# Rows of eight attention units loaded ahead into buffers that the dense layers have not yet filled, with a new written-out order

## The chip, the cores and the metric

The kernel runs on one core of a Trainium2 chip. The metric is the device time of one execution in microseconds (us). The engines work side by side, each through its own list of instructions: TensorE (PE, matmuls), VectorE (DVE), ScalarE (ACT), GpSimd (POOL) and SyncE (SP, which here only issues transfers). They wait for one another through semaphores.

## The reference

```python
# q, k, v: (8, 8, 576, 64); x: (4608, 512); w_in: (512, 2048); w_out: (2048, 512)
def attn(q, k, v):
    # 1: rows averaged in groups of 4, softmax attention over the 144 averages, result repeated 4 times
    # 2: softmax attention of each row over the rows with |i - j| < 4
    return out_up + out_local
x = attn(q, k, v).transpose(0, 2, 1, 3).reshape(4608, 512)
h = x @ w_in
out = (h - tanh(h)) @ w_out
```

All of it is float32 outside; the kernel casts to bf16 ahead of its matmuls.

## The kernel before

**Units.** Attention runs in 32 units. Unit p is the head pair p % 4 of batch p // 4. For each unit SP issues two loads of 256 KB (`load_qk`, L341: rows of k and of q, four sequence rows on one partition, into a buffer `st`) and two of 160 KB (`load_v`, L365: overlapping row windows of v for the two heads, into a buffer `vst`). The last 64 rows of q and k of a whole batch come in two loads of 128 KB (`sr`, L353), those of v in one (`vr`, L380). There are 4 buffers `st` and 5 buffers `vst`: unit p takes p % 4 and p % 5, so a load waits until the casts of the unit that had the buffer have read it.

**A unit's steps.** `st` is cast to bf16 (`qr`, L499; the last rows `rr`, L489), turned on PE for units 0 to 7 (L506) and by a transposing transfer on SP's queue from unit 8 on (L550; last rows L544), and pooled (L598 to L602, L613, L587, L592). `prep_v` casts `vst` (`vw`, L425), PE pools it (L456, units 0 to 11). PE makes the scores (L650, L660, L666), ACT the exponentials (L671 to L679), DVE or POOL the band mask (L706), PE the outputs (L720), DVE the division (L736, L738). The result goes back through PE (L763) or a transfer (L775) and is joined into `xT` (L756).

**Dense layers.** Block kb is one batch's 512 tokens. `mm1` (L797) multiplies `w_in` with `xT`, ACT takes tanh (L809) and DVE subtracts into `gT` (L812), two buffers by the block's parity. Block 0 multiplies `gT` with `w_out` directly (`mm2`, L878); blocks 1 to 7 use seven half products (L1018) on sums of `w_out` (`Tw`, four tiles, L927) and of `gT` (`S0` and others, L953). The weights come in 8 chunks of 1 MB issued by POOL (L406, L410).

**Order.** Nothing is scheduled on the chip or by the compiler. `Plan.emit` issues all operations in the order of the string `TURNS`; `ENGINES` says which engine takes an operation that has a choice, `BANKS` which PSUM bank, `FILL` where PE runs matmuls whose result is not used (L1227), and `BEHIND` adds waits between operations that share a port. Each engine works strictly in its own part of that order, and an SP transfer that has to wait holds back all that stand behind it on SP.

Of the kernel before, what the change touches and what calls it, by code (L numbers as in the profile page):

```python
# [7 lines left out]
FP32 = mybir.dt.float32  # L8
# [93 lines left out]
def kernel(  # L102
# [13 lines left out]
    NP = H // 2  # L116
# [38 lines left out]
        "000E0F0I0J06020B0M0N030K0L0G0H0401050O0P0Q0R0D0A0W0X0U0V0e0f101d1e11131B0g0h1512141f1g16"  # L155
        "171H1P0Y0Z180C0S0T1I1J1Q0k0l1C1A1L1K19220c0d1M1D1R1S091N1T1u231w0i0j1U2R1O1V240a0b252T26"
        "2G2H1v1j1k08291x1y2Z1l1m27200y1W0o0p071z1E2S1n1o2y2a280m0n1F2U211X1G2b1Y2c2X1Z2V1p1q2d39"
        "0z2I2J2z2W1r5H2n2o1a2Y1s2p2q0q0r3A1b2A2g1c1h1i0s0t3B2B3N3O2e2C3D33303P3Q3C2O1t2t2u3E312P"
        "2D2M2N0u0v3F3G352v2E2f5I2w363H325J343I5L3J37385P5K2K2L5M2h5N2Q5S5O2i2j5U665Q3K5R2F682k5E"
        "3L5v3M2l5T632m5x5V3d5F5X3j643k5y3p5w3q3r5B3s5C613e5D5z3t3v3w5W3l603m3f623u3g3T3U655Y3n3x"  # L160
        "3h0w0x3o6e3y6g3i412r2s426U43475Z3z6c4D3R3S5a444849456T674E6b46694F4G5g5h6B4A406d5b4B4J4K"
        "5c3V3W4P5d4H4L4M4C4Q3X3Y4R5k5l4N6V4I6X5e5f6W4S4V6Y4b5m5n6Z6f4O4T4c4d6a4e2x4h4U7A4i4j4f4W"
        "6A4X4Y4g5s4Z4k4n4o4l4a4t4u5G4v5t4z4w3Z3a4m6C6h6j556i506D4p6E4x514q526Q4r4y7D536F4s567B7F"
        "576G586H7f3b3c6R8854597C7g895A728d7E5u6k7I71967G6l976m7H6y8e6z8E8j8F8k737J76779C7K6n7L7l"
# [24 lines left out]
        "LnQyOgLvLzLoM0RTNfRDRELiM6NyOeOfR0M7LwM1RBRCMCMDM8M2O3O4QoMLMEM9O9OAMMOqOXOYOZMFMNOvRURV"
        "QuP0MOQzP1OoOkOiOjP6OlNZNaOrQvOhOsNXNYR1P9RFRGOpOwOmSJSKOxOtPER9RAOnR2RYPFRlRmPKOuOyO5O6"  # L190
        "P2PPRWP3RHRIP7R3P4RnRoOzV1PARXV2PBP5RNPGR4PHRZR5PCPLPIPSS4PDR6R7PMPTPJPNRaRORPRQPUPYRzRb"
        "PdPVRtPZPORyPeRcPaPRP8S0S1PWPfS5PlRePbPmSURpRqPXOBPgV3RLRMS6PnPqOcOdSWS7PvPoSNSOPrRdRrRs"
        "PwPsMSMTQ3RuPxQ4PtR8PcQ5PyQ8PhQ9Q6SPQFQAV5RfSRSSSAQBQGSVQKS2RgSQSZSaQLQHSdQPQMQIQQRvRwRx"
        "PjRhPiSXSYPkS3PpQNQYV6SLSMPuQRSeQES8PQQZPzSfQaQ1QSQ0V7V8ShQ2QpQ7QbQCVUSjRiRjQJSgS9QOQTSH"
        "SISbRRSBQDVBMHMIQdV9QUSqSrT6VAVCSCTTSDQeScQXSiSESFQcQhTRQfQiT7TUVTT8SyQjTZSzTaVZQgVDT9VE"
        "VVVWVOTETSUbVFTFVHSsStUcTgQkQlTGTHThSkTMVGTwV4TPTQTxSlVPSmTNTOU2VaU3VQVRUhRkU8VIVXSnSoUA"
        "VJVYVuUBVKUGUHTfVvVbUMTiSGVfTjVoVcUOVpToUPVdSpVqVrSTTpVwTvT2T0T1VxT3SuSvVeUiVySwSxUUT4Vz"
        "UVVLVMTuVgT5UNVsTAW0UaTBTIVmVhViTJVnTVTKU9TWUnVjVkW1TXTLUqTCW9UoUpUrVtTbQVQWTDTcWAW2TkW3"
        "TdTlW7UwTYTmWBVNTnUxWDTqWCTeVSW4W5TyUyTrWFW8U4WETsTzUCTtVlU0WGU1U5UDW6WHWIUIUEUJU6UQUFWJ"
        "WKURUKU7UWUXULUzV0USUdUYUTUeUjUfUZWLUsUkUgUtWSUuWXUlWcUvWMUmWTWUWQWYWNWZWRWeWaWfWOWmWsWV"  # L200
        "WPWdWxWWWiX4WbWgX5WtWhWkWyXAWzWnWuWlX0XFWoXGWjWpXNWqX6XOXSX7XXWvXPWrWwXHXBXIXYXCXfXZXTXD"
        "XkXaXgXlXQXrXhXwY1X1XiX3XUX8XqXVY2X2XxX9XEXvXJXsXyYAYBXmXzXLXMXnXRXWY0XbYOY3YFXcXdXtY4Y5"
        "XKXeY6YPXjXuXoYbYCY9YGYdYHXpYEYJYDY7Y8YQYKYIYRYSYLYTYUYcYMYNYVYeYWYfYiYgYZYaZ2YXYYYjYkYw"
        "YxZ3YyZ4YhYzYlZ0YmYnZ5Z1YoYpZ7YqZ6YrZAZ8Z9YvYsZBYtYuZCZDZJZEZKZHZFZGZOZIZPZQZRZSZLZMZN"
    )
    ENGINES = (
        "DDDDADDAAPPDAAPADADADDDDPDDDDDADPDAPDPDDAADPADAAAPADAAADDDDDDAPAADAAPPPDDDPPADAAAPPPPDAA"
        "PPADADPPPPDDPPPPAAPPPPDAAAADPPDADDAADDDDAPPPDDPPDADAPPAAPPDDAAPPPAAPPDDPPADDDDDPPDAPPAAP"
        "PDPDDAPPAAPPDPPPADPAADPDDPPADPPAADDDDPPDDDDDPPPAPPAADPDPDPAPPAADDDPDDAPPAAPPDDPPAPPPAAPD"
        "PDPPADDDDDPPPAPPAADPDPDDAPPAAPPDPDPADPAADDDPPPAPPPAADDDPPDDDDDDPPPAPPAAPPDPPPAPPDAPPDDPD"  # L210
        "APPAAPDDDPPAPPPDAPDDDDPADDDDDPPPAPPAAPPDPDPPDPAAPPDPPPDPAAPPDPPPPPDPDPPPDADDDDD"
    )
    BANKS = (
        "0123456017206457012760113005223301301030203210230101210031212003321100112311002032011320"
        "3101102201310203110023210201301001012110130100113200123101231023110021010131032110321321"
        "0301120310120031021101001002101021130203110032103213120130120310120120012010112030110210"
        "1010030210301230102310230123674512365714327601524736120"
    )
    FILL = (
        "13715 1771 1L61 1w31 2431 1E01 1X72 3351 3H21 2h72"  # L220
    )
    BEHIND = (
        "1B11 2S0y 5H0z 2f3F 655W 7A6a AmAF AnAL BiAs EgCZ DFFo JSFt IvGb IrJ6 MYJN MfJc NBKu QmL"
        "A LqNn NcNr O8OQ RYOp V1P7 SUS5 R8Ru Q0PQ VPVG VuRk VpVo UNVz VlWE"
# [60 lines left out]

    P = Plan(TURNS, ENGINES, BANKS, FILL, BEHIND)
# [51 lines left out]
    def load_qk(p):  # L338
        b, h0, s = p // NP, 2 * (p % NP), p % NST
        for n, src in enumerate((k, q)):  # L340
            load(500, lambda n=n, src=src: nc.sync.dma_start(  # L341
                out=st[s][:, n], in_=src[b, h0:h0 + 2].rearrange(
                    "h (g c) d -> g h (c d)", c=4)[0:128]),
                [("st", s, n)], 1000, 10 * p - 3000)
# [14 lines left out]
    def load_v(p):  # L359
        b, j, s = p // NP, p % NP, p % NVST  # L360
        for i in range(2):
            base = v[b, 2 * j + i]

            def issue(i=i, base=base):
                nc.sync.dma_start(out=vst[s][:, i], in_=bass.AP(  # L365
                    tensor=base.tensor, offset=base.offset,
                    ap=[[D, 128], [STEP * D, NT], [1, D]]))
            load(500, issue, [("vst", s, i)], 940, 10 * p - 3000 + 5)
# [52 lines left out]
    def prep_v(p):  # L421
        s, w = p % NVST, p % NVW
# [4 lines left out]
           reads=[("vst", s, 0), ("vst", s, 1)], writes=[("vw", w)])  # L427
# [831 lines left out]
```

## Time and profile before

| | |
|---|---|
| time, three runs | 314.4, 316.26, 320.43 us, median 316.26 |
| the profiled execution | 313.24 us, its span 311.5 us |
| granted TensorE clock, mean | 0.999 |
| PE busy | 299.8 us (96%), 2982 matmuls |
| DVE, ACT, POOL busy | 248.4 (80%), 213.4 (68%), 167.4 us (54%) |
| transfers | 60.81 MB, mean 195 GB/s |

The profiled execution took 3.0 us less than the median of the three runs. The span runs from the first instruction to the last. The views used below are the page's busy shares, the busy time of each engine by stretch (windows), the chain of waits that ended last, and the timeline of single engines.

### The profile page before, as it was taken

The numbers are of one execution on the slowest core, as the hardware profiler recorded it, in microseconds if no ns is written. First come the engines' busy times: TensorE is split into PE (matmuls) and PEld (weight loads), VectorE is DVE, ScalarE is ACT, GpSimd is POOL, SyncE is SP. The second block draws the span as 40 slices with busy tenths as digits, with TensorE's granted clock in tenths as the row PEclk, the third lists the DMA queues.
The fourth block names the chain that finished last, engine by engine and source line by source line (L and its number), as shares of the span: only waits on it lengthen the run. The fifth ranks groups of instructions, "written<-read, shape, count | busy, mean of one in ns | idle before, by whom it ended". The sixth has DMA issues, their size and how long they took to land.

```text
span 311.5 us, 7779 instructions
## 1 busy us (share of the span) xinstructions
PE 299.8 (96%) x2982; PEld 198.2 (64%) x2982; DVE 248.4 (80%) x443; ACT 213.4 (68%) x378; POOL 167.4 (54%) x222
## 2 busy tenths in 40 slices
PE   6898999999899999999999999999999999999994
PEld 2575555554477655875587755656878655468783
DVE  3888875689988988998998978977995888564944
ACT  2888883289778887889886788888947675554110
POOL 5198869046684368338771379387624582911200
PEclk9999999999999999999999999999999999999999
DMA  6999999599998999989999999999999653000224
GB/s 208 266 269 239 219 240 186 137 258 260 222 227 238 281 182 257 258 154 233 262 288 262 242 230 177 242 260 252 150 184 196 151 171 93 3 0 2 100 71 136
DMA packets 120870, 60.81 MB, mean 195 GB/s; under 512 B 88832, under 2 KB 118528, under 8 KB 120832
## 3 DMA queue, kind: packets, MB, share of 16 engines
q1 hardware_dynamic: 115968, 55.53, 78.8%
q0 software_dynamic: 4224, 4.19, 8.1%
q10 hardware_dynamic: 640, 0.59, 0.6%
q8 instruction: 23, 0.38, 0.5%
q14 instruction: 15, 0.12, 0.1%
HBM read 44.04 MB, written 9.44 MB: 172 GB/s over the span
## 4 chain that ended last, share of the span: by engine, by line
PE 83%; DMA 7%; POOL 5%; SPq 1%; issue 1%; DVE 0%; ACTq 0%; POOLq 0%; DVEq 0%
PE ps L797 32%; PE ps L1018 28%; PE ps L720 5%; PE ps L850 4%; PE ps L878 4%; PE ps L824 4%; PE ps L650 2%; DMA vst<-in_v_dram 2%; DMA st<-in_q_dram 2%; DMA sr<-in_q_dram 2%; DMA kq<-qr 1%; POOL qr L499 1%; PE ps L666 1%; PE ps L763 1%; POOL qkd L592 1%
## 5 line engine op out<-in xcount | busy, mean ns | idle before, releaser
L797 PE MATMUL ps<-xT,w_in_sb 128*128 128x512 bf16 x512 | 121.4, 379 | 0.0
L812 DVE TENSOR_TENSOR gT<-ps,u 128x512 bf16<-128x512 f32 x128 | 84.9, 686 | 21.6 <-ACT u L809 21.0
L809 ACT ACTIVATE u<-ps 128x512 f32<-128x512 f32 x128 | 74.2, 599 | 29.8 <-PE ps L797 25.0
L797 PEld LDWEIGHTS <-w_in_sb 128*128 128x128 bf16 x512 | 47.7, 98 | 47.9
L1018 PEld LDWEIGHTS <-gT 128*128 128x128 bf16 x672 | 64.1, 98 | 15.6
L1018 PE MATMUL ps<-w_out_sb,gT 128*128 128x256 bf16 x336 | 43.4, 273 | 0.0
L1018 PE MATMUL ps<-Tw,gT 128*128 128x256 bf16 x336 | 42.3, 273 | 0.0
L499 POOL CAST qr<-st 128x512 bf16<-128x512 f32 x49 | 29.8, 616 | 16.4 <-DVE vw L1156 6.1
L671 ACT ACTIVATE E<-ps 128x912 bf16<-128x912 f32 x32 | 29.7, 930 | 9.1 <-PE ps L660 6.7
L738 DVE TENSOR_TENSOR ln<-ps,r 128x768 bf16<-128x768 f32 x32 | 30.6, 957 | 1.2 <-DVE r L736 0.2
L1089 POOL TENSOR_TENSOR y<-y,keep 128x512 f32<-128x512 f32 x12 | 15.2, 1273 | 26.1 <-ACT y L1039 15.0
L577 ACT COPY kt<-kq 128x576 bf16<-128x576 bf16 x23 | 27.2, 1187 | 1.7 <-DMA kq<-qr 1.5
L587 POOL TENSOR_TENSOR half<-kq 128x576 f32<-128x576 bf16 x16 | 20.4, 1276 | 13.4 <-ACT kq L572 5.5
L720 PEld LDWEIGHTS <-E 128*128 128x128 bf16 x576 | 21.4, 97 | 6.2 <-POOL E L706 1.5
L592 POOL TENSOR_TENSOR qkd<-half 128x288 bf16<-128x288 f32 x20 | 16.5, 823 | 13.0 <-DVE r L736 5.8
L679 ACT ACTIVATE E<-ps 128x576 bf16<-128x576 f32 x32 | 21.0, 655 | 1.8 <-PE ps L666 1.8
L706 DVE TENSOR_TENSOR E<-E,mask 128x1152 bf16<-128x1152 bf16 x26 | 20.2, 785 | 1.4 <-ACT E L671 0.7
L837 DVE TENSOR_TENSOR gL<-ps,u 128x512 bf16<-128x512 f32 x16 | 15.9, 1020 | 5.2 <-ACT u L835 5.2
L756 POOL TENSOR_TENSOR xT<-lT 128x336 bf16<-128x336 bf16 (+1 forms) x26 | 17.0, 678 | 5.2 <-DMA lT<-ln 3.1
L720 PE MATMUL ps<-vw,E 128*128 128x65 bf16 x320 | 19.0, 193 | 0.7 <-POOL E L706 0.7
L1039 ACT COPY y<-ps 128x512 f32<-128x512 f32 x19 | 11.1, 587 | 11.9 <-PE ps L1018 11.6
L425 ACT CAST vw<-vst 128x640 bf16<-128x640 f32 x24 | 17.6, 731 | 1.1 <-DMA vst<-in_v_dram 1.1
(122 smaller groups left out, 470.5 us busy)
## 6 DMA issues: line engine op xcount, KB each, us to landing
vst<-in_v_dram SPq DMA_DIRECT2D x64, 160.0 KB, 4.4
st<-in_k_dram SPq DMA_DIRECT2D x32, 256.0 KB, 4.4
st<-in_q_dram SPq DMA_DIRECT2D x32, 256.0 KB, 4.5
out_dram<-y SPq DMA_DIRECT2D x14, 512.0 KB, 3.3
v<-in_v_dram SPq DMA_DIRECT2D x20, 256.0 KB, 4.5
w_in_sb<-in_moe_w_in_dram POOLq DMA_DIRECT2D x4, 512.0 KB, 10.7
w_out_sb<-in_moe_w_out_dram POOLq DMA_DIRECT2D x4, 512.0 KB, 7.9
vr<-in_v_dram SPq DMA_DIRECT2D x8, 128.0 KB
```

The source lines that it names most:

```text
L499: (eng, ns, lambda dst=dst, src=src, fn=fn: fn(out=dst, in_=src), port)
L577: ("ACT", 1180, lambda: A.copy(out=ktv, in_=src), False),
L587: eng.tensor_tensor(out=half, in0=flat[:, 0:576], in1=flat[:, 576:1152], op=ALU.add)
L671: A.activation(out=E[s][:, :, E0:E0 + 456], in_=at(s1)[:, :, PS0:512], func=AF.Exp, scale=SCALE)
L679: A.activation(out=E[s][:, :, EP:EW].rearrange("p h (i c) -> p h i c", i=2)[:, :, :, 0:G], in_=at(s2)[:, :, 120:408].rearrange("p h (i c) ...
L706: eng.tensor_tensor(out=el, in0=el, in1=mask.unsqueeze(1).to_broadcast([128, 2, S]), op=ALU.mult)
L720: T.matmul(po[:, hh, 65 * n:65 * n + 65], E[s][:, hh, e:e + 128], vv, start=start, stop=stop)
L738: op("DVE", 960, lambda: V.tensor_tensor(out=ln[s].rearrange("p n (h d) -> p h n d", d=D), in0=blocks()[:, :, :, 0:64], in1=r[s].unsqueeze ...
L797: T.matmul(at(name)[:, 0, :], w_in_sb[:, dc, fc * 128:(fc + 1) * 128], xT[dc][:, c0:c0 + S].rearrange("p (c g) -> p c g", c=4)[:, :, 0:128 ...
L809: op("ACT", 600, lambda: A.activation(out=u[us], in_=at(name)[:, 0, :], func=AF.Tanh), reads=[("hd", kb, fc)], writes=[("u", us)], uses=[n ...
L812: op("DVE", 690, lambda: V.tensor_tensor(out=gT[g][:, fc, :], in0=at(name)[:, 0, :], in1=u[us], op=ALU.subtract), reads=[("hd", kb, fc), ( ...
L1018: T.matmul(dst, left[:, f, 128 * j:128 * j + 128], right[:, f, :], start=(first and e == 0 and f == 0 and (j == 0 or apart)), stop=(e == 1 ...
```

## The change

The buffers `st` grow from 4 to 8 by using the four tiles `Tw`, which are first written when block 1 begins; the buffers `vst` grow from 5 to 9 by using three pieces of `gT[1]` (feature columns 13 to 15, 10 to 12, 7 to 9) and `S0`. Units 4 to 7 load q and k into the former `Tw`, units 5 to 8 load v into the latter. From unit 8 (q, k) and unit 9 (v) on the old buffers rotate as before. Dependencies keep the dense layers' first write behind the casts that read the guests. All of `TURNS`, `ENGINES`, `BANKS`, `FILL` and `BEHIND` are new; the number of operations is the same. The unused matmuls fall from 26 (15 of them at the start) to 24 (17 at the start).

```diff
+    st += [t.rearrange("p (n h a) x -> p n h (a x)", n=2, h=2).bitcast(FP32) for t in Tw]
+    g1 = gT[1].rearrange("p f x -> p (f x)")
+    vst += [a.bitcast(FP32).rearrange("p (h t d) -> p h t d", h=2, t=NT) for a in
+            [g1[:, 512 * f:512 * f + 4 * NT * D] for f in (13, 10, 7)] +
+            [S0.rearrange("p f x -> p (f x)")[:, 0:4 * NT * D]]]
+    def seat_qk(p):
+        return p if p < 2 * NP else p % NST
+    def seat_v(p):
+        return p if p < 9 else (p - 9) % NVST
+    LENT = {5: [("lent", f) for f in (13, 14, 15)], 6: [("lent", f) for f in (10, 11, 12)],
+            7: [("lent", f) for f in (7, 8, 9)], 8: [("lent", "S", e) for e in range(2)]}
...
-        b, h0, s = p // NP, 2 * (p % NP), p % NST
+        b, h0, s = p // NP, 2 * (p % NP), seat_qk(p)
...
-        b, j, s = p // NP, p % NP, p % NVST
+        b, j, s = p // NP, p % NP, seat_v(p)
...
-           reads=[("vst", s, 0), ("vst", s, 1)], writes=[("vw", w)])
+           reads=[("vst", s, 0), ("vst", s, 1)] + LENT.get(p, []), writes=[("vw", w)])
...
-           reads=[("hd", kb, fc), ("u", us)], writes=[("gT", g, fc)], uses=[name])
+           reads=[("hd", kb, fc), ("u", us)], writes=[("gT", g, fc)] + ([("lent", fc)] if kb == 1 else []), uses=[name])
...
-                   writes=[("T", n, e)], port=True)
+                   writes=[("T", n, e), ("st", NST + n, e)], port=True)
...
-                reads, writes = [], [("S", n, e) for e in es]
+                reads, writes = [], [("S", n, e) for e in es] + ([("lent", "S", e) for e in es] if n == 0 and kb == 1 else [])
...
-        "13715 1771 1L61 1w31 2431 1E01 1X72 3351 3H21 2h72"
+        "15717 2b71 2A71 3B41 2D11 5S31 3H31 6671"
```

The first transfers on SP in both orders (unit numbers; "v 0a" is one head's half of unit 0's v):

```
before  k0 vr q0 k1 q1 k2 v0a k3 sr1k q3 sr1q q2 v0b v2a v1a v2b v1b k5 k4 q4 v3a v4a v3b v4b q5 k6 q6 vr1 ...
after   q0 k0 q1 k1 k2 k3 vr v0 q2 q3 v1 v0 v3 v2 k4 sr1q v1 v2 q5 k5 v3 sr1k q4 v4 v4 k6 vr1 q6 v5 v5 ...
```

Here sr1 stands for the last rows of batch 1. On DVE the masks of units 0 to 3 all stand in the order after; before, those of units 1 and 2 were on POOL.

More of the change, by code (lines that the diff above doesn't have):

```diff
@@ L160 @@
[L160 to L164, printed above, removed]
@@ new lines @@
+        "0V171H1P18141I0B1J190m0n1L1Q1A1K1R221M1N0i0j1O242R231T1j1k1B251S1C1f1g1u1U0c0d1W1v1w2S1y"
+        "0k0l1x2Z091V2I2J0y2T082G2H1z1D2V291E2W0o0p261F1d1e2U1X1l1m212X27201n1o2z1Y2b1Z0z391p1q2a"
+        "0q0r2d282c2n2o1r1G2e311h1i1s2f2p2q2g2A2K2L322Y1t3A3B2B2O2y5H2C3C3D302D2P3G5I332E1a353E0s"
+        "0t2M2N5J34362v2h2F373N3O5K5L5P2i1b5e5f380u0v3F5M5S2w5N2r2s2j5O5Q3H5U5R3I3J5v662Q2k683K5B"
+        "5T1c635E5V3L3d2l5C5x2m643j3k5y3M3l3e5D5F3f3g5X3p3q5W0w0x3m3h3v3r3n3w3i3P3Q5w3s5Y3t2t2u3o"
@@ new lines @@
+        "413x615k5l3y3u5z3z4243604744404D4E4548623T3U495Z654A464F4G4B4J6b5a4K4H4L4M3V3W674N4C6e4P"
+        "6c6B4Q5g5h4I4R4S2x694V3R3S4O4W6g4b5b6T4X4c5c6A4T4Y5d4h5s4Z4U6V4i6U4j5t5m5n4k4a4d4e4l4n6W"
+        "3X3Y4o4f4p4q4m6C6d4r6X6D4t6Z4u6E6Y4v7A4w4z6a505G4g51526F7B536f6G554s4x3Z3a56576Q6j6H3b3c"
+        "587f7C6h7g6R54597D7E4y887F6i8d7G895A7I7H8e6k5u966l976m6y9C736z6n717J7475728E7K7l7L7m7677"
+        "8F8j8k6I6J7M8p6K6L7N8K7O5q5r7r6o6p5o5p7s78CC8L9t9u797xCE6u6v8q8v5i5j9f8w6q6rCF8Q8x6w6x8R"
@@ L208 @@
[L208 to L211, printed above, removed]
+        "APADDADAADPPDDPPDDADDDDAPPDADDAADDDPDDDDDAADDAPAADDDAAADDDPPAPPPAADAPPPDDDAAPADADPPPPDAA"
+        "PADAAAPPPDDAPDPDAAPPDPDAAAADPPAADDAADDDDDPDPDDPPDAAAPPAAPPDDAAPPPAAPPDDPPADDDDDPPPAPPAAP"
@@ L225 @@
+        "BP8 SVSU SdSW V6V5 R8TR RkVZ VmVz VlWE"
     )
```

105 lines of the change are left out of this document (51 added, 54 removed).

## The prediction

> **What bounds the kernel now.** I read the busy shares first, then the windows (columns: stretch, its length, busy us of PE, PEld, DVE, ACT, POOL with instruction counts, granted clock, DMA share, GB/s).
>
> ```profile
> PE 299.8 (96%) x2982; PEld 198.2 (64%) x2982; DVE 248.4 (80%) x443; ACT 213.4 (68%) x378; POOL 167.4 (54%) x222
> ...
> 0.00:10.00 10.00, 7.37 (x55) 3.96 (x56) 4.58 (x23) 3.84 (x8) 5.42 (x20) 1.00 0.79 228
> 10.00:20.00 10.00, 8.02 (x142) 6.21 (x140) 8.30 (x23) 8.08 (x18) 3.87 (x4) 1.00 1.13 261
> 20.00:30.00 10.00, 8.76 (x149) 6.38 (x146) 8.31 (x23) 8.58 (x20) 9.90 (x13) 1.00 1.19 248
> 30.00:40.00 10.00, 10.00 (x86) 5.15 (x84) 8.80 (x19) 8.38 (x18) 6.73 (x10) 1.00 1.22 226
> 40.00:50.00 10.00, 10.00 (x85) 5.20 (x84) 7.84 (x17) 7.38 (x15) 8.69 (x8) 1.00 1.20 237
> 50.00:60.00 10.00, 10.00 (x95) 5.66 (x95) 5.19 (x13) 0.91 (x2) 4.32 (x5) 1.00 0.70 134
> 60.00:80.00 20.00, 19.77 (x171) 10.02 (x169) 17.69 (x35) 17.79 (x32) 10.12 (x14) 1.00 1.12 231
> 80.00:120.00 40.00, 38.38 (x417) 26.64 (x414) 35.51 (x58) 31.62 (x55) 23.99 (x33) 1.00 1.10 238
> 120.00:160.00 40.00, 40.00 (x429) 27.30 (x428) 36.38 (x59) 33.95 (x60) 24.36 (x33) 1.00 1.02 234
> ...
> 280.00:311.00 31.00, 27.50 (x258) 22.89 (x256) 17.83 (x24) 6.38 (x12) 2.50 (x2) 1.00 0.24 78
> ```
>
> PE is the bound, and its idle time is in three places only: 5.85 us in the first 30 us (2.63 + 1.98 + 1.24), 1.85 us between 60 and 120, and 3.5 us at the end. The granted clock is 1.00 everywhere. From 30 us on no faster load can help except in that middle gap: where PE shows 10.00 of 10, work that comes sooner waits for PE. Transfers have a share above 1 from 10 to 50 us, so they are saturated in the very stretch into which the change brings loads forward; they fall to 0.70 from 50 to 60. The ceiling of any gain is the first gap and the middle one.
>
> The first gap, from the timeline of single engines (start, duration, engine, line; in brackets idle time before it and what ended it):
>
> ```profile
> 1.26 4.69 PE L1227 MATMUL ps<-lT 128*128 128x512 bf16 x15 [1.26 <-DVE lT L1149]
> 13.86 0.43 DVE L499 CAST qr<-st 128x512 bf16<-128x512 f32 x1 [0.98 <-DMA st<-in_q_dram]
> 14.34 0.40 PE L506 MATMUL ps<-ident,qr 128*128 128x128 bf16 x4 [1.32 <-DVE vw L1156]
> 14.44 0.64 ACT L489 CAST rr<-sr 128x512 bf16<-128x512 f32 x1
> 16.36 2.88 SPq L365 DMA_DIRECT2D vst<-in_v_dram  x4
> 22.09 1.16 DVE L706 TENSOR_TENSOR E<-E,mask 128x1152 bf16<-128x1152 bf16 x1 [0.35 <-ACT E L675]
> 23.34 2.38 POOL L706 TENSOR_TENSOR E<-E,mask 128x1152 bf16<-128x1152 bf16 x1
> 25.78 0.33 PE L720 MATMUL ps<-vw,E 128*128 128x65 bf16 x5 [0.69 <-POOL E L706]
> 28.56 0.95 DVE L756 TENSOR_TENSOR xT<-ps,od 128x336 bf16<-128x336 bf16 x4
> 29.39 1.89 PE L797 MATMUL ps<-xT,w_in_sb 128*128 128x512 bf16 x8
> ```
>
> Dense work begins at 29.39, when the last `xT` of batch 0 is being written (28.56 + 0.95 = 29.51). Two things hold that up: unit 2's q, twelfth transfer on SP, cast at 13.86, and unit 2's mask, which stood on POOL until 25.72 while DVE masks unit 3.
>
> The middle gap, from the chain that ended last (start, us, what), with the row of the timeline at its end:
>
> ```profile
> 73.17 0.61 POOL qr L499
> 73.78 0.57 POOL rr L489
> 74.35 1.62 SPq L550
> 76.01 0.57 SPq L341
> ...
> 77.14 6.20 DMA vst<-in_v_dram
> ...
> 84.23 0.45 PE L456 MATMUL ps<-vw,pick 128*128 128x128 bf16 x5 [1.45 <-POOL vw L425]
> 87.45 0.30 PE L666 MATMUL ps<-qkd 64*128 64x144 bf16 x4 [0.17 <-POOL qkd L592]
> ```
>
> SP's transposing transfer of unit 11 waits for POOL's casts; behind it on SP stands the second half of unit 11's v, which is issued at 77.14, lands at 83.34, is cast on POOL and releases PE at 84.23.
>
> **The change part by part.** No operation is added but waits; the cost lies in the orders.
>
> *Unused matmuls.* 26 become 24. One of 512 columns takes 0.216 us, from this row of the chain (24 in 5.18):
>
> ```profile
> 56.94 5.18 PE ps L878 x24
> ```
>
> Two fewer are −0.43 us at most; they stood in front of waits, so this is counted inside the next term and not again.
>
> *Start.* I follow the new order by hand with durations of before. These rows give them (last two numbers ahead of the bar's end: busy us, mean ns):
>
> ```profile
> L671 ACT ACTIVATE E<-ps 128x912 bf16<-128x912 f32 x32 | 29.7, 930 | 9.1 <-PE ps L660 6.7
> L738 DVE TENSOR_TENSOR ln<-ps,r 128x768 bf16<-128x768 f32 x32 | 30.6, 957 | 1.2 <-DVE r L736 0.2
> L706 DVE TENSOR_TENSOR E<-E,mask 128x1152 bf16<-128x1152 bf16 x26 | 20.2, 785 | 1.4 <-ACT E L671 0.7
> L679 ACT ACTIVATE E<-ps 128x576 bf16<-128x576 f32 x32 | 21.0, 655 | 1.8 <-PE ps L666 1.8
> vst<-in_v_dram SPq DMA_DIRECT2D x64, 160.0 KB, 4.4
> ```
>
> Unit 2's q is now the ninth transfer with 512 KB less ahead of it, so the wait at 14.34 mostly goes, and no mask is on POOL. But two new waits take their place. Batch 1's last rows of k move from the 9th to the 22nd transfer, and ACT's cast of them (14.44 before) still stands ahead of unit 3's exponentials. Issues 21 to 24 ran from 16.36 on, 2.88 us for four, with 4.4 us to land: the 22nd lands at about 16.9 + 4.4 = 21.3. Cast 0.64, exponentials 0.93 + 0.65 + about 0.35: unit 3 is ready for its mask at 23.8. On DVE the cast of unit 4's q, 23rd transfer, landing at 21.9, stands ahead of six small operations (about 1.9 us in all) and unit 3's mask: 0.43 + 1.9 bring the mask to 24.2 and its end to 25.0. Outputs on PE 0.55, then unit 2's and unit 3's divisions on DVE (0.96 each) end at 27.2, the way back through PE and two copies at 28.5, the joins (0.95 for two units) at 29.45. So the last `xT` is ready when it was before, but six dense matmuls on the other units' `xT` now stand in front of that wait: 6 x 0.216 = 1.3 us of work is done where none was. I take −1.2 us. Bounds: −3.1 us, if no wait but the opening ones remains in the first 30 us (5.85 less 1.26 less 1.5 for the first load); +2 us, if the two named loads land 2 us later than their predecessors in those positions.
>
> *Weights.* The second chunk of `w_in` moves behind three POOL casts. It is needed about 2 us sooner. What I know of its landing is this spread for equal chunks:
>
> ```profile
> 19.62 1.69 POOL L406 DMA_DIRECT2D w_in_sb<-in_moe_w_in_dram  x2
> 22.59 0.74 POOL L406 DMA_DIRECT2D w_in_sb<-in_moe_w_in_dram  x1
> 33.10 0.80 POOL L406 DMA_DIRECT2D w_in_sb<-in_moe_w_in_dram  x1
> DMA to landing us min/median/max: 7.3/10.7/13.6
> ```
>
> Before, the second was issued at 20.4. If it is issued at 23.5 (unit 3's v lands near 21, then three casts of 0.6 to 0.7) and needed at 31.5 (17th dense matmul, the first at 28.1), the minimum makes it early by 0.7 us and the maximum late by 5.6. I take 0, nearest to the minimum, because chunks go one behind another and the first is earlier now (POOL reaches it after fewer operations). 0 to +5.6 stays for the range.
>
> *Lent buffers.* SP's own stall of 14 us (40.99 to 54.44) is behind the first transposing transfer, not behind a buffer:
>
> ```profile
> 40.45 0.54 SPq L341 DMA_DIRECT2D st<-in_q_dram  x1
> 54.44 1.36 SPq L550 DMA_TRANSPOSE kq<-qr  x1
> ```
>
> In both orders that transfer comes after about 40 loads, and the loads of units 4 to 8 stand ahead of it in both, save that units 5 to 7 of v no longer wait for casts. Lending by itself is thus worth nothing on PE: cover is the direct product of block 0 (L878), which keeps PE at 10.00 from 50 to 60. POOL has two masks fewer in 40 to 52, so I expect the transfer some 3 us sooner; what that buys is slack, not time.
>
> *Middle gap.* Unit 11's second v half now stands ahead of unit 11's transposing transfer on SP, right behind unit 10's. Without the wait of 1.62 and what stands before it, it is issued near 73.5 in place of 77.14, 3.6 us sooner, and the cast is ready before PE needs it (82.8). −1.45 − 0.17 = −1.6 us. Next late is unit 9's v, issued behind unit 9's transposing transfer; by the 3 us of the last paragraph it lands just in time. Bounds: −1.85, all idle time from 60 to 120; +2, if the 3 us fail and unit 9's v, at 4.4 us to landing, is late by what is missing.
>
> *End.* The last 31 us keep their sequence of products; 0.
>
> Sum against the profiled execution: 313.24 − 1.2 − 1.6 = 310.44 us. The median of the runs shown, 316.26, lies 3.02 above that execution, and I add it: 313.5 us, 0.9% less. A measurement of this kernel, whose three runs spread by 6 us, tells about 2% from no change.
>
> **Rivals.**
> 1. *Weights starved: slower.* Loads that no longer wait are always in SP's queue while the weights come, and the second chunk of `w_in` lands at the maximum above: PE waits 5.6 us. 313.5 + 5.6 = 319.1. It decides once that chunk lands after 31.5. For: DMA share 1.19 to 1.22 and a spread of 7.3 to 13.6. Against: that spread arose with a full SP queue already. [...] If the same befalls the third or fourth chunk too, the time passes 322.6.
> 2. *Nothing but slack.* The two new waits (last rows of k, q of unit 4) eat the start and another wait replaces the middle gap: 316.3 − 0.4 = 315.9. For: PE full from 30 us on, transfers saturated. Against: both named gaps end in a load that moves forward.
> 3. *Slack shows in the other runs.* The profiled execution was 3.0 us below the median; if those 3.0 are late loads, and loads now have more lead, they go, and the start reaches its bound: 313.5 − 3.0 − 1.9 = 308.6. For: every gap named ends in a load. Against: no row shows what the slower executions waited for.
>
> **How the numbers follow.** Forecast 0.42, rival 1 0.18, rival 2 0.18, rival 3 0.22. Forecast's own range is 309 to 317: start −3.1 to +2, middle −1.85 to +2. The whole range goes from 307 (rival 3 with a bit of spread) to 321 (rival 1 with more than one chunk). Faster by over 2% means under 309.9: 0.19 of rival 3 and 0.05 of the forecast, 0.24. Slower by over 2% means over 322.6: 0.12 of rival 1 and 0.01 of rival 2, 0.13. Within: 0.63.
>
> **What would show it.** Right: first L797 (L814 by the new lines) at 28 to 28.5 with a wait for `xT` within its first 7; the rows of casts of sr (ACT) and unit 4's q (DVE) with idle time ended by a DMA near 21 to 22; no PE idle near 82 to 84; the first transposing transfer on SP near 51; PE idle outside start and end under 0.5 us. Wrong: a PE wait for `w_in` between 31 and 40 (rival 1), the first dense matmul after 30, or a new PE wait for v or the transposed q between 55 and 90 (rival 2). All of it fails if PE shows idle time after 120.

## The result, and the profile after

| | before | after |
|---|---|---|
| median over 22 executions each | 315.17 us (312.93 to 326.13) | 311.32 us (310.3 to 314.8) |
| profiled execution, its span | 313.24, 311.5 us | 311.1, 309.4 us |
| ratio after to before | | 0.9894 [0.987, 0.9918] |

The changed kernel is 1.06% faster; the interval is a quarter of a per cent to either side and excludes no change. The forecast was 313.5 us, a change that no measurement would tell from none. The time lies in the forecast's range, but a change half as large would have been told from none. (The ratio leaves out executions over 1.5% above a kernel's fastest; medians and counts below are over all executions.)

The page and the windows of after, columns as in the prediction:

```profile
PE 299.1 (97%) x2969; PEld 198.6 (64%) x2980; DVE 248.2 (80%) x450; ACT 213.5 (69%) x380; POOL 165.0 (53%) x213
```

```profile
0.00:10.00 10.00, 8.45 (x57) 4.28 (x57) 4.06 (x24) 3.81 (x8) 5.52 (x19) 1.00 0.84 233
10.00:20.00 10.00, 7.52 (x130) 5.79 (x125) 7.26 (x21) 7.36 (x16) 3.47 (x5) 1.00 0.98 249
20.00:30.00 10.00, 7.88 (x147) 6.03 (x148) 7.73 (x20) 8.04 (x18) 6.41 (x11) 1.00 1.14 238
30.00:40.00 10.00, 10.00 (x84) 5.20 (x83) 8.72 (x20) 7.62 (x16) 7.87 (x11) 1.00 1.20 238
```

PE's 20 to 30 us are less full than before (7.88, then 8.76). The timeline of single engines shows what stands there:

```profile
21.98 0.62 ACT L506 CAST rr<-sr 128x512 bf16<-128x512 f32 x1 [0.94 <-DMA vst<-in_v_dram]
22.72 0.43 DVE L516 CAST qr<-Tw 128x512 bf16<-128x512 f32 x1 [0.56 <-DMA Tw<-in_q_dram]
23.48 0.38 PE L546 MATMUL ps<-ident,rr 128*128 128x128 bf16 x4 [0.75 <-ACT E L688]
24.52 0.42 DVE L533 COPY kq<-ps 128x512 bf16<-128x512 bf16 x1 [1.03 <-PE ps L523]
25.98 0.23 DVE L753 RECIPROCAL r<-ps 128x12 f32<-128x12 f32 x1 [0.60 <-ACT kq L583]
26.21 0.74 DVE L723 TENSOR_TENSOR E<-E,mask 128x1152 bf16<-128x1152 bf16 x1
30.16 0.38 PE L814 MATMUL ps<-xT,w_in_sb 128*128 128x512 bf16 x1
```

The casts of the two named loads start at 21.98 and 22.72 behind landings, 0.7 and 0.8 us later than the landings forecast for 21.3 and 21.9. The bracket of the first row names v; the chain that ended last has the k rows themselves there, issued at 17.36 and landed at 21.90:

```profile
17.36 4.54 DMA sr<-in_k_dram
```

Behind them DVE's copy at 24.52 and its reciprocal at 25.98 wait, and unit 3's mask starts at 26.21 where 24.2 was forecast; the first dense matmul starts at 30.16, before at 29.39. The forecast was 28 to 28.5, and a start after 30 was among its signs of being wrong.

The middle gap is gone. Windows of before, then of after:

```profile
80.00:85.00 5.00, 3.55 (x30) 1.96 (x27) 4.64 (x7) 3.32 (x8) 2.82 (x4) 1.00 1.24 272
85.00:90.00 5.00, 4.83 (x93) 4.22 (x91) 3.71 (x5) 4.17 (x7) 4.30 (x6) 1.00 1.15 282
```

```profile
80.00:85.00 5.00, 5.00 (x73) 3.66 (x73) 4.74 (x8) 4.47 (x10) 4.02 (x6) 1.00 1.22 283
85.00:90.00 5.00, 4.95 (x79) 4.08 (x80) 5.00 (x7) 4.67 (x9) 3.50 (x5) 1.00 1.05 238
```

**A measure for the rest.** Busy shares hide small waits, so I also work out PE's *lost time* at a moment: the start of the matmul there, less the columns of all matmuls issued before it at one fixed time for 512. That time is a yardstick of mine, about 1% under the 0.216 us of the prediction's row; no row shows it, so each figure also holds some of the work itself (with 0.216 the 2.6 of before from 95 to 300 is 0.1). Unused matmuls count as work; the two fewer are 0.43 us more for after. The traces of after, e17 and e18 lack 11 matmul records each (above: PE x2969 beside PEld x2980); these are counted in. Only differences between executions mean something. By stretch, in us, with two later profiled executions of each kernel (labels e12, e15, e16, e18 below):

| execution | to 32 us | 32 to 80 | 80 to 95 | 95 to 300 |
|---|---|---|---|---|
| before, 313.24 | 10.0 | 1.5 | 2.1 | 2.6 |
| before, 315.42 (e15) | 12.6 | 1.4 | 1.9 | 2.4 |
| before, 315.15 (e16) | 12.3 | 1.1 | 2.5 | 2.4 |
| after, 311.1 | 11.4 | 0.6 | 0.3 | 2.5 |
| after, 311.25 (e12) | 11.6 | 0.6 | 0.3 | 2.5 |
| after, 310.88 (e18) | 11.2 | 0.6 | 0.3 | 2.5 |

Between profiled executions the start *lost* 1.0 us (1.4 less 0.43), the stretch to 80 gained 0.9, the gap 1.8, and nothing changed from 95 to 300. But the execution of before that was profiled first had a lucky start: against the other two, the start gained about 1.5 with the unused matmuls, and of the five profiled executions with that order at the start (e1 with 10.6 and e2 with 13.7 besides these three) it has the smallest loss.

### The profile page after: what moved, and what is told of

Read it like the earlier page. It is cut to its first block, busy times and chain, and to the rows that moved or that the text cites. A ratio compares the mean times of both kernels' runs of the same rounds, so it can differ in the third digit from the quotient of the medians.

```text
span 309.4 us, 7786 instructions
## 1 busy us (share of the span) xinstructions
PE 299.1 (97%) x2969; PEld 198.6 (64%) x2980; DVE 248.2 (80%) x450; ACT 213.5 (69%) x380; POOL 165.0 (53%) x213
## 4 chain that ended last, share of the span: by engine, by line
PE 90%; DMA 3%; SPq 3%; DVE 1%; issue 1%; ACT 0%; DVEq 0%; ACTq 0%
PE ps L814 36%; PE ps L1035 28%; PE ps L737 5%; PE ps L841 5%; PE ps L867 4%; PE ps L895 4%; PE ps L667 3%; SPq L382 2%; DMA st<-in_k_dram 2%; DMA sr<-in_k_dram 1%; PE ps L780 1%; PE ps L683 1%; SPq L358 1%; PE ps L473 1%; PE ps L677 1%
## 5 line engine op out<-in xcount | busy, mean ns | idle before, releaser
L516 POOL CAST qr<-st 128x512 bf16<-128x512 f32 x40 | 24.1, 615 | 20.6 <-DVE gT L970 6.2
L723 DVE TENSOR_TENSOR E<-E,mask 128x1152 bf16<-128x1152 bf16 x29 | 23.5, 813 | 1.4 <-ACT E L688 0.7
L773 POOL TENSOR_TENSOR xT<-lT 128x336 bf16<-128x336 bf16 (+1 forms) x24 | 15.9, 684 | 14.8 <-DMA st<-in_k_dram 4.7
L604 POOL TENSOR_TENSOR half<-kq 128x576 f32<-128x576 bf16 x15 | 19.2, 1281 | 5.9 <-DVE v L454 1.8
L737 PE MATMUL ps<-vpr,E 128*128 128x65 bf16 x128 | 16.3, 194 | 0.0
```

The lines of the kernel that those rows point to most:

```text
L516: (eng, ns, lambda dst=dst, src=src, fn=fn: fn(out=dst, in_=src), port)
L604: eng.tensor_tensor(out=half, in0=flat[:, 0:576], in1=flat[:, 576:1152], op=ALU.add)
L723: eng.tensor_tensor(out=el, in0=el, in1=mask.unsqueeze(1).to_broadcast([128, 2, S]), op=ALU.mult)
L737: T.matmul(po[:, hh, 65 * n:65 * n + 65], E[s][:, hh, e:e + 128], vv, start=start, stop=stop)
```

## The experiments

Moves are shown on the order in which SP or another engine issues, in the names of the list of first transfers ("k4": rows of k of unit 4).

### Lending, and one edit at a time

**e1: the buffers are lent, the five strings stay those of before.**

```diff
 st, vst, seat_qk, seat_v, LENT: as after
-TURNS, ENGINES, BANKS, FILL, BEHIND: as after
+TURNS, ENGINES, BANKS, FILL, BEHIND: as before
```

> The order of before, all five strings, with the lent buffers alone. Theory (lending is worth nothing on PE, the order is what counts): within 0.5 us of before, same first dense matmul near 29.4 and the gap of 1.45 us at 82.8 to 84.2 still there. Rival (loads that need not wait for a buffer are the gain): most of the 3.9 us between the medians, and that gap gone.

Measured: 315.95 us median of 10, ratio to before 0.9976 [0.9926, 1.0026]. Lending alone moves nothing that can be measured; most of the change's time lies in the order. The details of the expectation were not met: in the profiled execution (312.83 us) the first dense matmul started at 29.93, and the gap at 84.2 was 0.56 us, not 1.45. So that gap varies in an unaltered order, or lending shortens it; one execution does not tell which.

**e2: before, with unit 11's second v half ahead of unit 11's transposing transfer.**

```diff
 SP of before, near 74 us
-v11a, transposing transfer of unit 11, ..., v11b
+v11a, v11b, transposing transfer of unit 11, ...
```

> Before with one SP transfer moved: the second half of unit 11's v ahead of unit 11's transposing transfer. Nothing else changes on any engine. Theory (that wait is a term of its own): the gap at 82.8 to 84.2 goes, 1.6 to 1.8 us less. Rival (something else is late there too): the gap stays or moves, less than 0.5 us.

Measured: 314.06 us median of 10, ratio 0.9981 [0.9938, 1.0025]. The gap went (0.4 us lost from 80 to 95), but the median did not follow. The profiled execution, 316.57 us, is the slowest of the ten and shows what made it slow; its waits near 25 us and its windows:

```profile
ACT qr L499 <- DMA st<-in_q_dram: 4.5, 1, 4.5
PE ps L506 <- ACT qr L499: 2.9, 1, 2.9
```

```profile
24.00:26.00 2.00, 1.10 (x23) 0.82 (x21) 1.59 (x4) 0.00 (x0) 1.98 (x2) 1.00 1.17 243
26.00:28.00 2.00, 0.01 (x1) 0.01 (x1) 0.21 (x1) 0.68 (x2) 0.53 (x1) 0.80 1.18 243
28.00:30.00 2.00, 2.00 (x20) 1.45 (x21) 0.42 (x1) 1.97 (x6) 0.65 (x2) 0.50 1.18 246
30.00:32.00 2.00, 2.00 (x33) 1.73 (x31) 1.48 (x4) 1.31 (x4) 1.92 (x4) 0.50 1.18 246
32.00:34.00 2.00, 2.00 (x22) 1.58 (x21) 1.62 (x7) 1.29 (x3) 2.00 (x4) 0.50 1.18 245
34.00:36.00 2.00, 2.00 (x16) 1.06 (x14) 1.62 (x4) 1.65 (x5) 0.10 (x1) 0.99 1.21 277
```

One load, the q rows of unit 5, landed 4.5 us after ACT was ready for it. PE stood still for 2.9 us, and the granted clock fell to 0.50 until 34: the lost time to 32 us is 13.7, not 10.0. From here on I held theory A: late rows at the start, with a lowered clock behind them, make most of the difference between the medians. Theory B: the difference is the sum of fixed steps that single profiled executions show.

**e3: after, with the same v half put back behind the transposing transfer and the load that follows it.**

```diff
 SP of after, near 73 us
-v11b, q12, k12, transposing transfer of unit 11, v13a
+q12, k12, transposing transfer of unit 11, v13a, v11b
```

> After with the same transfer put back behind unit 11's transposing transfer and one more load. Theory: a PE gap ahead of unit 11's v pooling comes back, 1.0 to 1.8 us more than after. Rival (the new order has enough lead elsewhere): no change within 0.3 us.

Measured: 310.87 us median of 4, ratio 0.988 [0.9803, 0.9957]; no gap came back (0.2 us lost from 80 to 95), with the v half issued at 75.68 us (before: 77.14, after: 73.32). So the place of this one transfer is not what closes the gap in after; its whole order on SP is ahead there. The expected 1.0 to 1.8 us did not come.

**e4: after, with the last k rows of batch 1 and unit 4's q issued sooner, unit 5's q later.**

```diff
 SP of after
-k4 sr1q v1 v2 q5 k5 v3 sr1k q4 ...
+sr1k k4 sr1q v1 v2 q4 k5 v3 q5 ...
```

> After with three SP transfers moved: batch 1's last rows of k from 22nd to 15th, unit 4's q from 23rd to 20th, unit 5's q behind it. Theory (ACT's and DVE's waits for these two loads hold up unit 3 and with it the first dense matmul): both waits go, the first dense matmul comes 0.9 us sooner, 0.9 us less in all. Rival (batch 0's own v, now later by 0.4 us, or PE's order holds the start): no gain, or up to 0.5 us more.

Measured: 311.1 us median of 10, ratio 0.9929 [0.9892, 0.9966]: no gain. In the profiled execution (313.52 us) another load was late, the last v rows of batch 1, on which DVE waited 2.4 us, and the granted clock was 0.69 from 30 to 32 us and 0.50 from 32 to 34. Inconclusive on the term it was to test; e13 does it better.

### Splices, and the margin of one row

The two orders hold the same operations, so one's start, up to the first dense matmul, can be joined to the other's remainder.

**e5 and e6: start of one order, remainder of the other.**

```diff
 e5: TURNS, ENGINES, BANKS, FILL, BEHIND
+first 229 operations as before, the others as after
 e6:
+first 226 operations as after, the others as before
```

> The changed kernel's code with the five written strings spliced: every operation up to the first dense matmul (229 operations, with their engines, banks and unused matmuls) in the order of before, all later ones in the order of after. Theory A (the window of the weights): the two kernels differ in their medians mostly because rows of the first stage that are still in SP's queue when the first piece of w_in begins to move, near 22 us, land 3 to 5 us later, all engines wait, and the granted clock then falls to half for some us; the order of before is exposed to that, the order of after is less so. Then this kernel keeps the wide spread of before: median 313 to 314.5 against about 314.5 of before in the same call (only the gap near 82 us is gone, worth about 1), and a third of its executions with a granted clock under 0.997. Theory B (fixed sums): the difference is what the profiled executions show, gap near 82 us -1.8, 32 to 80 us -0.9, end -0.35, start +1.0. Then this kernel keeps all of the gains and drops the loss: about 311.4 (3.1 under before), and it would beat after.

> The mirror splice: the first 226 operations (up to the first dense matmul) in the order of after, all later ones in the order of before. Theory A: few executions with a lowered clock, median 312 to 313, that is 1.5 to 2.5 under before, though the gap near 82 us may return. Theory B: the start's +1.0 without the gains, 315 to 315.5, slower than before.

Measured: e5 313.14 us, ratio 1.0015 [0.9973, 1.0056]; e6 316.65 us, ratio 1.0037 [0.9985, 1.0088]. Neither splice is faster than before. e5 lies in A's range (unit 5's q late by 3.9 us in its profile, the gap gone, 0.3 us; but 7 of 10 executions with a lowered clock, where A gave a third); B's 311.4 is refuted. e6 misses both: its start is after's (11.4), but in its profiled execution the remainder of before brought the gap back larger than in any other. At 319.37 us that is the slowest of the ten and not typical. Its chain and windows:

```profile
80.13 6.79 DMA vst<-in_v_dram
86.92 0.02 issue
86.94 0.02 POOLq L441
86.96 0.08 issue
87.04 1.62 POOL vw L441
```

```profile
86.00:88.00 2.00, 0.00 (x0) 0.00 (x0) 1.85 (x3) 0.09 (x1) 0.96 (x1) 1.00 1.10 205
88.00:90.00 2.00, 1.30 (x13) 1.30 (x13) 1.25 (x2) 0.57 (x2) 2.00 (x3) 0.60 1.11 317
90.00:92.00 2.00, 2.00 (x23) 2.00 (x21) 0.24 (x1) 1.37 (x2) 2.00 (x4) 0.54 1.15 271
```

Unit 11's v took 6.79 us, PE stood from 85.5 to 88.7, and the clock fell to 0.60 and 0.54 in the last two rows: 5.1 us lost from 80 to 95 instead of 2.1 (and 3.0 from 32 to 80, which I did not take apart).

**e7: before, with unit 5's q ahead of all four v transfers of units 3 and 4.**

```diff
 SP of before
-v3a v4a v3b v4b q5
+q5 v3a v4a v3b v4b
```

> Before with one issue moved: SP issues the q rows of unit 5 ahead of the four v transfers of units 3 and 4 instead of behind them, some 3 us sooner (about 16.5 instead of 19.3 us), so that they land well before the weights begin to move near 22 us. Theory A, if this row is the one that most often misses the window (in the profiled execution of the second experiment it landed at 27.30 instead of 23.17, and the clock then fell to 0.50): median 312.5 to 313.5, 1 to 2 under before, and fewer executions with a granted clock under 0.997 than the 8 of 25 that before had. Theory B: nothing, 314 to 315. If the late row is now another one (the v rows that were passed), the share of lowered clocks stays as it was.

Measured: 315.24 us, ratio 1.0047 [1.0011, 1.0083], slower, so A's 312.5 to 313.5 is missed. The passed v rows were now late (POOL waited 1.1 us for unit 3's), the case that the expectation named last.

**e8: after, with unit 4's q behind unit 4's two v transfers.**

```diff
 SP of after
-q4 v4 v4
+v4 v4 q4
```

> After with one issue moved: SP issues the q rows of unit 4 behind the two v transfers of unit 4 instead of ahead of them, about 1 us later. Theory A: the rows now cross the weights' start, land near 24 to 26 us instead of 22, ACT's cast waits 2 to 4 us for them, the first dense matmul starts at 31 to 33 us, and the granted clock falls in many executions: median 313 to 315, 2 to 4 over after's 311.3. Theory B: a row 1 us later is at most 1 us of loss, 311.5 to 312.3, clock at 1.0.

Measured: 316.8 us, ratio 1.007 [1.0027, 1.0112], 5.5 us over after's median for one row's place in SP's list. Its waits and windows:

```profile
DVE qr L516 <- DMA Tw<-in_q_dram: 4.5, 1, 4.5
PE ps L523 <- DVE qr L516: 3.1, 1, 3.1
```

```profile
24.00:26.00 2.00, 0.00 (x0) 0.00 (x0) 0.00 (x0) 0.38 (x2) 0.00 (x0) 1.00 1.15 262
26.00:28.00 2.00, 1.34 (x26) 1.34 (x27) 1.61 (x6) 0.68 (x2) 1.28 (x2) 0.88 1.17 290
28.00:30.00 2.00, 2.00 (x24) 1.19 (x21) 1.01 (x5) 1.15 (x5) 1.42 (x3) 0.50 1.16 250
```

This is theory A's mechanism in one move: a row issued at 18.76 instead of 18.04 kept DVE waiting 4.5 us instead of 0.56, and the clock fell in all 10 executions (means of 0.984 to 0.995). The median lies above A's own 313 to 315, and B is refuted.

### Mending before

**e9: before, with unit 4's v behind unit 5's q. e10: that, and e2's edit. e11: e9's edit on the splice e5. e12: after, unaltered, on the same chip.**

```diff
 SP of before (e9, e10) and of the splice (e11)
-v3a v4a v3b v4b q5
+v3a v3b q5 v4a v4b
```

> Before with the two v transfers of unit 4 issued behind the q rows of unit 5 instead of ahead of them; the v transfers of unit 3, which POOL needs first, stay where they were. The rows of unit 5 are issued 1 us sooner (about 18.3 instead of 19.3 us). Theory A (rows caught behind the weights at 22 us, then a lowered clock): the rows of unit 5 land before the weights begin to move, the first dense matmul starts at 29 to 29.5 us, median about 313, 1 under before; what spread is left is that of the wait for unit 11's v near 82 us. Theory B (fixed sums): no change, 313.5 to 314.5. If unit 4's v now becomes the late row, the median is 1 to 2 over before.

> The edit just named and, besides, the last v half of unit 11 issued ahead of unit 11's transposing transfer, as in the second experiment. Theory A: with both late landings mended the order of before should do what the changed order does: 311 to 312.2, 2 to 3 under before and within 0.3% of the changed kernel. Theory B (the gain lies in the whole new order, 32 to 80 us and the end included): 313 to 314 as in the second experiment.

> The splice (start in the order of before, all later operations in the order of after) with unit 4's v transfers behind unit 5's q rows. Theory A: a start of before's length without its late row (about 10 us of loss by 30 us) and after's remainder (about 3.5): 309.8 to 311, at or a little under the changed kernel. Theory B, or a start that is late in another row: 312.5 to 313.5 as the splice without the move.

> The changed kernel itself, unaltered, so that the other three are compared with it on the same chip and against the same runs of before: 311 to 311.6, ratio to before 0.987 to 0.993.

| | median of 12 (e12: 9) | ratio to before | clock lowered in |
|---|---|---|---|
| e9 | 314.7 us | 0.9967 [0.9925, 1.0009] | 5 of 12 |
| e10 | 313.12 us | 0.9961 [0.992, 1.0003] | 2 of 12 |
| e11 | 313.79 us | 0.9964 [0.9923, 1.0005] | 10 of 12 |
| e12 | 311.25 us | 0.9924 [0.9885, 0.9964] | 3 of 9 |

All three miss A's figures (about 313, 311 to 312.2, 309.8 to 311), and no interval of the three excludes no change. e10 lies in B's 313 to 314, and e9 and e11 lie 0.2 and 0.3 us over B's ranges. So the two late places that A named are not enough. e10's profiled execution, the fastest of its twelve, took 311.07 us, as little as after's, by two moves on SP (lost: 9.9, 1.4, 0.2, 2.5 by stretch). One execution of before can thus be brought to after's time; its median, 1.9 us over after's, cannot with these two moves. A third exposed place is seen in the traces, though no run mends it alone: in nine of the ten profiled executions that start in the order of before PE stands 1.3 to 1.7 us at 13 us, ahead of unit 2's first transposes (the prediction's row at 14.34, put there to unit 2's q), and in e9, e11 and e15 the clock fell within 1.1 us behind it or in it (0.51 from 16 to 18 us in e9, 0.61 and 0.68 from 14 to 16 in e11 and e15). Windows of e15:

```profile
14.00:16.00 2.00, 1.00 (x10) 1.01 (x11) 1.49 (x5) 1.31 (x4) 0.00 (x0) 0.68 0.80 162
16.00:18.00 2.00, 2.00 (x17) 1.44 (x15) 1.47 (x5) 0.33 (x2) 1.70 (x2) 0.50 0.90 250
18.00:20.00 2.00, 2.00 (x46) 1.62 (x45) 0.94 (x2) 1.66 (x4) 1.23 (x1) 0.97 1.08 313
```

The new order issues unit 2's q ninth instead of twelfth, and no profiled execution with its start has that standstill.

### The start's failed term, the unused matmuls, and before again

**e13: after, with ACT's cast and PE's transposes of batch 1's last rows later.**

```diff
 ACT of after
-cast sr1, exponential E0 of unit 3, E2, E1
+E0, E2, E1 of unit 3, cast sr1
 PE of after
-transposes sr1, way back of unit 0, transposes q4, transposes k5
+way back of unit 0, transposes q4, transposes k5, transposes sr1
```

> After with ACT's cast of batch 1's last rows put behind unit 3's three exponentials and PE's transposes of them behind the transposes of units 4 and 5 (two operations moved, nothing else). If those transposes are what held unit 3's mask back in the changed kernel: unit 3's mask starts near 24.5 to 25.3 us instead of 26.2, the first dense matmul at 29.0 to 29.6 instead of 30.16, median 310.2 to 310.8. Rival: unit 4's rest columns, which need the moved transposes, come late instead, and the first dense matmul stays at 30 to 30.5: 311 to 311.8.

Measured: 310.7 us median of 6, ratio 0.9914 [0.9891, 0.9937], clock never lowered. In the profiled execution (311.53, the slowest of the six) unit 3's mask started 2.90 us behind the cast of unit 4's q, but then DVE stood for another load ahead of the joins, and the first dense matmul started at 30.61, later than after's 30.16:

```profile
22.44 0.43 DVE L516 CAST qr<-Tw 128x512 bf16<-128x512 f32 x1 [0.73 <-DMA Tw<-in_q_dram]
...
25.34 0.78 DVE L723 TENSOR_TENSOR E<-E,mask 128x1152 bf16<-128x1152 bf16 x1
...
29.83 0.29 DVE L404 TENSOR_TENSOR vrs<-vr 128x128 f32<-128x128 f32 x1 [1.59 <-DMA vr<-in_v_dram]
30.04 0.52 DVE L773 TENSOR_TENSOR xT<-ps,od 128x336 bf16<-128x336 bf16 x2
```

In the six profiled executions that have after's order there (after, e3, e6, e12, e14, e18) the distance from that cast to that mask is 3.5 to 3.7 us, in e13 and e17 it is 2.9: the two moved operations are worth 0.6 to 0.8 us there. The distance is the better measure, because the landing itself varies; e18, unaltered:

```profile
21.27 0.49 DVE L516 CAST qr<-Tw 128x512 bf16<-128x512 f32 x1 [0.35 <-DMA Tw<-in_q_dram]
...
24.82 0.74 DVE L723 TENSOR_TENSOR E<-E,mask 128x1152 bf16<-128x1152 bf16 x1
```

**e14: after, without the seven unused matmuls inside the start.**

```diff
-"15717 2b71 2A71 3B41 2D11 5S31 3H31 6671"
+"15717"
```

> After without the seven unused matmuls inside its start (one each ahead of seven of its operations); the 17 at the opening stay. If they stand in PE's waits and keep the clock from falling: more executions with a granted clock under 0.997 (after had 2 of 22) and a median of 312 to 313.5. If they only fill time: 310.9 to 311.5, the same. If they delay the work behind them by their 0.21 us each: 310 to 310.8.

Measured: 313.13 us, ratio 0.9969 [0.9934, 1.0004], with the clock lowered in 7 of 12 (means of 0.989 to 0.995): 1.9 us slower than after by leaving out 1.5 us of work whose result nobody uses. The first alternative of the expectation holds. The clock is not all of it: the five executions without a lowered clock have a median of 311.73, after's 311.15.

**e15, e16: before, profiled twice more.**

```diff
 nothing changed
```

> Before itself, unaltered, profiled once more. Theory A (late rows at the start, a late v of unit 11 near 82 us, each at times followed by a lowered clock): against its first profiled execution (about 10.0 us of PE's time lost by 30 us, 2.1 between 80 and 90) it differs in these two stretches, by up to 3 us in each, and in all others by under 0.6 us together. Theory B: it differs everywhere a little.

> Before itself, profiled a third time. Theory A: it differs from the other two profiled executions of before up to 30 us and between 80 and 90 us, and elsewhere by under 0.6 us together. Theory B: it differs everywhere a little.

Measured: 315.42 and 315.15 us. The table above has their lost time: they differ from the first profiled execution by 2.3 to 2.6 us up to 32 us, by 0.2 to 0.4 from 80 to 95 and by under 0.6 elsewhere together, as theory A says. In e16 it is unit 5's q again. Its row, and the queues of transfers (q1 is SP's loads, q0 POOL's weights) at 18 to 20 us and at 24 to 26:

```profile
25.94 0.62 ACT L499 CAST qr<-st 128x512 bf16<-128x512 f32 x1 [3.02 <-DMA st<-in_q_dram]
```

```profile
q1 hardware_dynamic: 1048, 0.48, 96.6%
```

```profile
q0 software_dynamic: 238, 0.24, 73.1%
q1 hardware_dynamic: 189, 0.19, 36.1%
```

Once the weights move, SP's queue carries 0.19 MB in 2 us instead of 0.48. In e15 the clock was 0.68 from 14 to 16 us (above), and the first dense matmul waited for `w_in`:

```profile
32.01 1.90 PE L797 MATMUL ps<-xT,w_in_sb 128*128 128x512 bf16 x8 [0.80 <-DMA w_in_sb<-in_moe_w_in_dram]
```

**e17: e13, with DVE's sum over batch 1's last v rows behind the joins, and POOL's half of unit 5 no longer behind that sum. e18: after, unaltered, on the same chip.**

```diff
 DVE of e13
-sum vr, joins xT of units 0, 2 and 3
+joins xT of units 0, 2 and 3, sum vr
 BEHIND
-... 5Q5N 635B 5w5W ...
+... 5Q5N 5w5W ...
```

> The kernel just tried (after with batch 1's last q and k rows cast and transposed later) and, besides, DVE's sum over batch 1's last v rows moved behind the last of the products xT that the first dense block needs, with POOL's half of unit 5 no longer made to wait for it. If the late landing in front of those products was what was left: no wait of DVE for vr before the first dense matmul, first dense matmul at 28.8 to 29.8 us, loss by 32 us 10.3 to 11.0, median 309.8 to 310.6. Rival: batch 1's column pool comes late for unit 4's output matmuls, and the wait stands there: 310.7 to 311.3.

> The changed kernel itself, unaltered, for the direct comparison on one chip: 311.0 to 311.6, ratio to before 0.988 to 0.993, so that the other kernel stands 0.2 to 0.5% under it if its late sum was the cause.

Measured: 310.69 us (8 executions, 310.01 to 312.53, clock never lowered) against 311.06 us (6, 309.97 to 311.83), ratios to before 0.9887 [0.9847, 0.9928] and 0.9895 [0.9856, 0.9935]. The first dense matmul came 0.5 us sooner (e17, then e18):

```profile
29.43 0.38 PE L814 MATMUL ps<-xT,w_in_sb 128*128 128x512 bf16 x1
```

```profile
29.93 0.38 PE L814 MATMUL ps<-xT,w_in_sb 128*128 128x512 bf16 x1
```

e17 beats before; its median is 0.1 us over the expected 309.8 to 310.6, and the 0.37 us under e18 are not told apart by these runs.

## Why the prediction was right or wrong

**The step that failed: what a measurement can tell, and the 3.02 us added to the sum.** The sum for the profiled execution was 310.44; it took 311.1. Then 3.02 us, the distance of the median of three runs, was carried over unchanged. Over 22 executions that distance is 1.9 us before and 0.2 us after. The excess was no noise of the chip that any kernel would have, since after on the same chips does not show it: in the slower executions of before that were profiled, loads landed late (unit 5's q in e16, unit 2's q and `w_in` in e15). That was rival 3, which had 0.22; it is about half right (the excess went, the start did not reach its bound). And an excess with a cause does not set the limit of what can be told: 2% was read off a spread of three runs, and 22 executions of each kernel told a quarter of a per cent. The sum itself came within 0.7 us by luck: the start missed by 2.2 us the one way, and the gap, 32 to 80 and the end by 1.5 the other. And the bounds stated for the start and the gap do not give the stated range: with the 3.02 us they run from 311.3 to 320.3, not from 309 to 317.

All executions whose clock is listed, by whether the mean granted clock was under 0.996 (a lowered clock, below):

| | executions | with lowered clock | median without | median with |
|---|---|---|---|---|
| before | 118 | 51 (43%) | 313.75 us | 315.89 us |
| after | 37 | 6 (16%) | 311.15 us | 312.84 us |

The rarer lowered clock is thus worth about 0.5 us (27% of some 2 us) of the 2.9 us between these pooled medians (314.12 and 311.25); 2.6 us remain between executions with a full clock. The table by stretch shows where those lie: 1.6 to 2.2 at the gap, 0.5 to 0.9 from 32 to 80, and the start from a loss of 1.0 to a gain of about 1.5, by the execution.

**Start, −1.2: wrong against the profiled execution (+1.0), and by its own step.** The mask came 2.0 us late (26.21 for 24.2), and from there to the first dense matmul it took as long as forecast (3.95 us for 3.9). Of the 2.0 us, 0.8 is the landing of unit 4's q, which varies (its cast started at 22.72 here, at 21.27 in e18). The other 1.2 us is the step "six small operations (about 1.9 us in all)", which took them as ready: from the start of that cast to the mask it gave 2.3 us, and 3.5 to 3.7 were measured in all six executions with after's order. The copy among the six waits for PE, which stood behind the transposes of batch 1's last rows (23.48); these waited for ACT, and the reciprocal by its row for ACT's copies of the same rows. e13 and e17 moved the cast and the transposes, and the distance fell to 2.9: shown for 0.6 to 0.8 us of the 1.2 or more. That the term comes near −1.5 against ordinary executions of before is not to its credit.

**Middle gap, −1.6: right in place and size** (1.8). Its reason was right only in part: the first transposing transfer came at 54.17, not near 51 (before 54.44), so the 3 us of lead are not there; and e3 shows that in after the moved v half is not needed for it. e2, and e10 with e9's edit beside it, show that on before's order the move closes it.

**Weights, 0; rival 1: no PE wait for `w_in` in after**, as forecast, but by luck. Rival 1 was to decide once the second chunk lands after 31.5, and it did. Its issue in after, and the landing of the four chunks:

```profile
23.83 0.75 POOL L423 DMA_DIRECT2D w_in_sb<-in_moe_w_in_dram  x1
```

```profile
DMA to landing us min/median/max: 8.8/9.4/10.9
```

It landed at 32.6 at the earliest (23.83 + 8.8). PE did not wait, because the 17th dense matmul, which needs it first, started at 34.40 and not at the forecast 31.5: the late start hid it. A start as early as forecast would have met a wait of at least 1.1 us. The reverse of rival 1 is in both kernels: once the weights move, SP's queue carries less. In e16 it falls from 0.48 MB at 18 to 20 us to 0.19 at 24 to 26, beside 0.24 in the weights' queue; in after from 0.62 at 18 to 20 to 0.12 at 22 to 24, beside 0.24. So the rows in SP's queue come late too. A forecast that had also asked what the weights do to the rows might have found part of the spread of before.

**Lent buffers, 0: right** (e1). **Unused matmuls: the sum counted only their 0.43 us**; in e14 leaving out the seven inside the start cost 1.9 us, in part by a lowered clock, in part by something that stays open. **32 to 80, forecast 0: gained 0.5 to 0.9**, from no single wait that I found; this stays open. **End, 0: right** to about 0.3 us. Also open: executions of before with a full clock still run from 311.35 to 316.28, and three profiled ones show late loads, not that every slow one has them.

## What to carry to other kernels

Where a median lies well above the profiled execution, profile again until a slow one is caught, before its excess is added to a forecast as if it were fixed: here 1.7 of the 3.85 us between the medians lay in that excess. In a stretch with saturated transfers (a DMA share of 1.15 to 1.17 in e8 from 24 to 30 us) look for loads issued just before another queue begins to move; a place or two in the list decided here between a wait of 0.6 us and one of 4.5 (e8). A wait of PE costs more than its length if the clock falls behind it (in e2 2.9 us, then 0.50 from 28 to 34 us), so a few unused matmuls in front of such waits can be worth more than they take (e14).

## What the runs showed of the hardware

The lowest granted clock in these rows is 0.50, and lowered stretches differ in length. In e2 the rows from 26 to 36 us fall short of a clock of 1.00 by 2 x (0.20 + 0.50 + 0.50 + 0.50 + 0.01) = 3.42 us; in e15, from 14 to 20, by 2 x (0.32 + 0.50 + 0.03) = 1.70, half as much.

The length of one standstill does not tell here whether the clock falls. It fell in or behind standstills of PE of 1.8 us (e4), 1.69 (e15), 1.46 (e9) and 1.3 (e11), and in e14 near 29 us with no standstill over 1.01. It stayed up after 1.66 (e16, at 84.75 us), 1.45 (before, at 82.8 us), 1.43 (e16) and 1.3 (e10). The rows of e14, and the one of e16 with 1.66, around which the granted clock is 1.00 from 82 to 92 us:

```profile
28.00:30.00 2.00, 1.38 (x18) 0.80 (x14) 1.94 (x6) 1.12 (x2) 1.71 (x3) 0.76 1.22 222
30.00:32.00 2.00, 2.00 (x14) 1.38 (x13) 1.82 (x7) 0.69 (x2) 2.00 (x4) 0.50 1.22 195
```

```profile
86.41 0.45 PE L456 MATMUL ps<-vw,pick 128*128 128x128 bf16 x5 [1.66 <-POOL vw L425]
```

What decides whether the clock falls was not shown.
